# The last piece's keys in two halves of four steps, and the last half's store in three parts by lanes

## The chip, the cores and the metric

The kernel runs on one core of a Trainium2 chip (trn2). The metric is the device time of one execution in microseconds (us), before and after the change, as the median of several runs. A core has five engines with a queue of instructions each: TensorE (PE, matmuls and transposes), VectorE (DVE), ScalarE (ACT), GpSimd (POOL) and SyncE (SP, which here only starts DMA transfers). Each engine takes its instructions in order and waits on semaphores for the others.

## The reference

The computation has three stages, one behind the other. The change lies in the first.

```python
# attention-like recurrence: batch 4, 8 heads, 768 steps, head dimension 48; a = a_re + i*a_im
mag = sqrt(a_re^2 + a_im^2);  scale = min(mag, 0.999) / (mag + 1e-6);  a_n = a * scale
for t in range(768):
    S = a_n[t] * S            # complex, rows scaled
    S.re += outer(k[t], v[t])
    y[t] = q[t] @ S.re
# x = y as (3072 tokens, 384); then a mixture of 8 experts, top 1
e = argmax(x @ w_gate);  out = gate * (relu(x @ w1[e]) @ w2[e])
# then a gated product
h = (x @ w1) * (x @ w2);  out = (h @ w3) @ w_out
```

The kernel writes the recurrence in chunks of 64 steps. Within a chunk it takes the running products P of the decays; a query is multiplied by P and a key by the conjugate of P over |P|^2 (called "keys" here), so that a chunk becomes a masked product of queries and keys, and the state is carried from chunk to chunk.

## The kernel before

The 768 steps are three groups (g) of four chunks. 128 lanes hold 2 pairs of batches (q), 4 chunks (c), 8 heads and the 2 batches of a pair, in that order, so that 16 lanes belong to one (q, c). Two streams are written side by side by `drive`, which takes the next step of the stream that is behind in estimated time (the numbers that the steps yield).

**Stream 1, `elementwise`**, works on 24 pieces of 8 steps (`TP`), eight for each group; piece i covers 8 steps of all 128 lanes. For a piece: `root`, `excess` and `norm` make the scaled decays; `prefix` makes P one step after the other, each step a product (line 893, tile `pr`) and a sum (line 895, tile `P`) on DVE that needs the step before; `power` squares P on ACT (line 900, tile `s`); `weigh` adds the two squares (line 837, on DVE for the pieces of the last group) and takes 1/|P|^2 as Ln and Exp on ACT (lines 909, 910); `keys` multiplies on DVE (lines 918, 920, 922) and makes the tile `qk` with all products of a piece in one instruction of 1536 elements a lane (line 925). A piece's `qk` goes to `qkd` in HBM. The pieces that end a group (`LAST`: 7, 15, 23) are stored from SP in two halves of 64 lanes (line 934), the others from POOL (line 936). `keys` of a piece is written down two rounds after its `prefix`, except for a group's last piece, where it comes one round after it.

**Stream 2, `groups`**, works on units (g, q, c). `loads` (line 1027) reads a unit's 16 lanes and 64 steps back from `qkd` as tile `kk`, 768 KB in rows of 768 bytes; PE transposes it (line 1011, tile `tr`), multiplies it into scores and outputs (lines 1039, 1058, 1059), and carries the state in `W` (lines 1096, 1103). A group's first load needs the store of the group's last piece: `yield lambda: self.made > LAST[g]`. Behind it, when the units of a group have given their rows, `route` picks experts and scatters rows to HBM from POOL (line 162, after `pi` on DVE, line 157).

During the third group a side stream splits weights (`Fuse`, tiles `fdr`, `fdm`), which SP loads behind the first three `kk`. Then come the experts (lines 350 to 352, PE) and the last product.

Which instruction stands where in an engine's queue is settled when the program is built: a list scheduler with a model of time takes, for each engine, the earliest instruction in program order that is ready in the model. So an instruction that is written later can stand in a gap of one that is written earlier.

Of the kernel before, what the change touches and what calls it, by code (L numbers as in the profile page):

```python
# [9 lines left out]
F32 = mybir.dt.float32  # L10
# [4 lines left out]
AF = mybir.ActivationFunctionType  # L15
ALU = mybir.AluOpType
# [81 lines left out]
def bc(ap, n, at):  # L98
    shape = list(ap.shape)
    return ap.unsqueeze(at).to_broadcast(shape[:at] + [n] + shape[at:])  # L100
# [520 lines left out]
NH = 8  # L621
SEQ = 768
D = 48
C = 64
NG = 3
TP = 8
NPC = C // TP
NPIECE = NG * NPC
# [14 lines left out]
LAST = {g: max(r for r, x in enumerate(PAIRS) if g in [y[0] for y in x]) for g in range(NG)}  # L643
R2 = 2 * D
# [12 lines left out]
LAG = 5000  # L657
REST = 3
ZB = 4
HP = 1000  # L660


# [130 lines left out]
class Attn:  # L793
# [33 lines left out]
    def elementwise(self, aside, factors):  # L827

        nc, S, ep, e2 = self.nc, self.S, self.ep, self.e2
        v, act = nc.vector, nc.scalar  # L830
        E = TP * D
        td = lambda ap: ap.rearrange("p (t d) -> p t d", d=D)
        a, sq, pu, y0, cf, P, s2, px, raw = ({} for _ in range(9))

        def add(i, nm, s):
            if i not in ADDS[nm]:
                v.tensor_tensor(out=s[0], in0=s[0], in1=s[1], op=ALU.add)
                return s[0]
            p = self.adds.tile([128, 512], F32, tag="ad", name=f"{nm}{i}", bufs=2)[:, :E]
            for r in range(2):  # L840
                nc.tensor.matmul(p, S.ident, s[r], start=r == 0, stop=r == 1)  # L841
            return p

        def root(i):
            sq[i] = x = ep.tile([128, 2, E], F32, tag="sq", name=f"sq{i}", bufs=AHEAD)
            act.activation(out=x, in_=a[i], func=AF.Square, accum_out=S.su[:, i : i + 1])
            pu[i] = add(i, "u", (x[:, 0], x[:, 1]))
            y0[i] = y = ep.tile([128, E], F32, tag="y0", name=f"y0{i}", bufs=AHEAD)
            act.activation(out=y, in_=pu[i], func=AF.Ln, bias=S.tiny[:, 0:1])
            act.activation(out=y, in_=y, func=AF.Exp, scale=-0.5)  # L850
            act.activation(out=x[:, 1], in_=y, func=AF.Square, accum_out=S.sy[:, i : i + 1])

        def excess(i):
            v.tensor_tensor(out=sq[i][:, 0], in0=pu[i], in1=sq[i][:, 1], op=ALU.mult)
            yield 470

        def norm(i):
            u, y = sq[i][:, 0], y0[i]
            v.scalar_tensor_tensor(out=u, in0=u, scalar=3.0, in1=y, op0=ALU.subtract, op1=ALU.mult, reverse0=True)
            act.activation(out=y, in_=y, func=AF.Identity, scale=-0.4995e-6, bias=S.wb)  # L860
            yield 470
            v.scalar_tensor_tensor(out=u, in0=u, scalar=2.0 / 0.999, in1=y, op0=ALU.min, op1=ALU.mult)
            yield 470
            cf[i] = c = ep.tile([128, TP, 4, D], F32, tag="cf", name=f"cf{i}", bufs=2)
            ar = a[i].rearrange("p r (t d) -> p t r d", d=D)
            v.tensor_tensor(out=c[:, :, 0:3:2], in0=ar, in1=bc(td(u), 2, 2), op=ALU.mult)
            act.activation(out=c[:, :, 1], in_=c[:, :, 2], func=AF.Copy, scale=-1.0)
            act.copy(c[:, :, 3], c[:, :, 0])  # L868
            yield 870

        def prefix(i):
            P[i] = e2.tile([128, TP, 2, D], F32, tag="P", name=f"P{i}", bufs=3)
            m = len(PAIRS[i])
            n = TP // m
            run = lambda x: x.rearrange("p (m t) r d -> p m t r d", m=m)
            c, o = run(cf[i]), run(P[i])
            for t in range(n):
                k = [k for k in range(m) if t or PAIRS[i][k][1]]
                for x in range(m):
                    if x not in k:  # L880
                        v.tensor_copy(o[:, x, 0], c[:, x, 0, 0:3:2])
                        yield 120
                if not k:
                    continue
                if t:
                    pv = o[:, :, t - 1]
                else:
                    old = len(PAIRS[i - 1])
                    pv = P[i - 1].rearrange("p (m t) r d -> p m t r d", m=old)[:, old - len(k) :, TP // old - 1]
                j = len(k)  # L890
                pr = e2.tile([128, 2, 2, 2, D], F32, tag="pr", name=f"pr{i}_{t}", bufs=1)[:, :j]
                cx = c[:, :j, t].rearrange("p m (w r) d -> p m w r d", w=2)
                v.tensor_tensor(out=pr, in0=cx, in1=bc(pv, 2, 2), op=ALU.mult)  # L893
                yield 100 + 170 * j
                v.tensor_tensor(out=o[:, :j, t], in0=pr[:, :, :, 0], in1=pr[:, :, :, 1], op=ALU.add)
                yield 70 + 100 * j

        def power(i):
            s2[i] = e2.tile([128, 2, E], F32, tag="s2", name=f"s2_{i}", bufs=2)
            act.activation(out=s2[i].rearrange("p r (t d) -> p t r d", d=D), in_=P[i], func=AF.Square)  # L900
            g, _, n = PAIRS[i][0]
            if i == LAST[g]:
                self.last[g] = l = self.st.tile([128, 2, 2, D], F32, tag="td", name=f"td{g}")
                act.copy(l, P[i][:, n - 1].unsqueeze(2).to_broadcast([128, 2, 2, D]))

        def weigh(i):
            px[i] = add(i, "x", (s2[i][:, 0], s2[i][:, 1]))
            g0 = s2[i][:, 1]
            act.activation(out=g0, in_=px[i], func=AF.Ln, bias=S.tiny[:, 1:2])
            act.activation(out=g0, in_=g0, func=AF.Exp, scale=-1.0)  # L910

        def keys(i):
            g, _, n = PAIRS[i][0]
            k = raw[i][:, :, 1]
            x, g0 = s2[i][:, 0], s2[i][:, 1]
            if i == LAST[g]:
                v.tensor_copy(S.xm[:, g], px[i][:, (n - 1) * D : n * D])
            v.tensor_tensor(out=x, in0=px[i], in1=g0, op=ALU.mult)
            yield 470
            v.tensor_tensor(out=k, in0=k, in1=td(g0), op=ALU.mult)  # L920
            yield 470
            v.scalar_tensor_tensor(out=k, in0=td(x), scalar=2.0, in1=k, op0=ALU.subtract, op1=ALU.mult, reverse0=True)
            yield 470
            self.qk[i] = o = self.qp.tile([128, TP, 2, 2, D], F32, tag="qk", name=f"qk{i}")
            S.end = v.tensor_tensor(out=o, in0=bc(P[i], 2, 2), in1=bc(raw[i], 2, 3), op=ALU.mult)
            yield 1740
            self.stored = self.qk.pop(i).rearrange("p t w r d -> p (t w r d)")
            at = 0
            for g, t, n in PAIRS[i]:
                dst = S.qkd[g].rearrange("q c h b t w e -> (q c h b) t (w e)")[:, t : t + n].rearrange("l t e -> l (t e)")  # L930
                src = self.stored[:, at * 2 * R2 : (at + n) * 2 * R2]
                if i == LAST[g]:
                    for l in (0, 64):
                        done = nc.sync.dma_start(dst[l : l + 64], src[l : l + 64])
                else:
                    done = nc.gpsimd.dma_start(dst, src)
                at += n
            with self.tc.issue_after(done.ins):
                aside(i)
            self.made = i + 1  # L940
# [21 lines left out]
        yield from chain(excess(0), norm(0), excess(1))  # L962
        for i in range(NPIECE + 1):
            if i:
                power(i - 1)
                weigh(i - 1)
            if i % 2 and i + 5 < NPIECE:
                a[i + 5], a[i + 6] = self.load_a(i + 5)
            if i + AHEAD < NPIECE:
                root(i + AHEAD)  # L970
            if i + 1 < NPIECE:
                raw[i + 1] = self.load_qk(i + 1)
            ends = [j in LAST.values() for j in (i - 2, i - 1)]
            rest = [keys(i - 2)] if i > 1 and not ends[0] else []
            if i + 1 < NPIECE:
                rest.append(norm(i + 1))
            if ends[1]:
                rest.append(keys(i - 1))
            if i + 2 < NPIECE:
                rest.append(excess(i + 2))  # L980
            yield from mix(*([prefix(i)] if i < NPIECE else []), chain(*rest))
            if i == NPIECE - 1:
                factors()
# [92 lines left out]
    def chain(self, u, ld):  # L1076
# [8 lines left out]
        v, kk = ld  # L1085
        z = st.tile([R2, 2, HD], F32, tag="z", name=f"z{nm}", bufs=ZB)
        first = g == 0 and c == 0
# [27 lines left out]
    def fill(self, cost):  # L1115
# [3 lines left out]
        while self.pool and spent < cost:  # L1119
# [14 lines left out]
            try:  # L1134
                with self.tc.high_priority(HP) if self.spare is not None else nullcontext():
                    c = next(x.steps)
# [316 lines left out]
```

## Time and profile before

| | us |
|---|---|
| median of 3 runs | 996.49 |
| lowest, highest | 995.11, 997.68 |
| the profiled execution | 997.66 |
| its span, first to last instruction | 996.0 |
| PE busy in it | 885.2 (89%) |
| DVE busy | 609.6 (61%) |
| ACT busy | 496.2 (50%) |

All times within the trace count from the first instruction of the span. A busy share is an average over stages; a wait counts where PE, the busiest engine, stands still. In a row of a timeline the columns are start, duration, engine, line, operation, tile written and tiles read, partitions x elements, and the number of instructions merged into the row; brackets at the end give the engine's idle time before it and what ended that.

### The profile page before, as it was taken

Reading aid. Unit: us, or ns where it says so; the run is one execution under the profiler, and the core shown is the slowest. Engines: PE = TensorE matmul, PEld = TensorE weight load, DVE = VectorE, ACT = ScalarE, POOL = GpSimd, SP = SyncE. Lnnn points to the kernel's source line nnn. Section 1 sums busy time; section 2 is a strip of 40 time slices with the busy share of each in tenths; the row PEclk is TensorE's granted clock in tenths of the full one; section 3 lists DMA queues with packets and bytes.
Section 4 is the critical chain, followed back from the end, with each engine's and each line's share of the span. In section 5 each row is a group of like instructions: output and inputs, shape, how many; then the busy total and the mean of one; then the engine's idle time right before and its main releaser. Section 6 shows DMA issues by size and latency. Waiting matters only on the chain. (4 is left out here: it accounts for less than half of the span.)

```text
span 996.0 us, 17046 instructions
## 1 busy us (share of the span) xinstructions
PE 885.2 (89%) x6386; PEld 759.2 (76%) x6386; DVE 609.6 (61%) x1373; ACT 496.2 (50%) x1113; POOL 133.8 (13%) x194
## 2 busy tenths in 40 slices
PE   3535899879993898999989999998999999999997
PEld 1212478667873787989979999997888888888886
DVE  6999999888994795676489995443232323232222
ACT  7556699868862775344456654443131313131211
POOL 6111000202031011100233211110010100000001
PEclk9666899989995999899999999999999999999999
DMA  7556975476636872653678745630000000000000
GB/s 249 180 188 238 283 253 180 136 222 209 184 129 186 275 225 90 190 183 113 196 218 192 202 111 136 139 66 2 1 16 16 16 17 12 21 9 25 9 24 32
DMA packets 90183, 128.75 MB, mean 129 GB/s; under 512 B 7232, under 2 KB 72688, under 8 KB 90096
## 3 DMA queue, kind: packets, MB, share of 16 engines
q1 hardware_dynamic: 76540, 83.79, 29.8%
q0 software_dynamic: 10448, 39.18, 11.2%
q10 hardware_dynamic: 3108, 4.65, 1.5%
q8 instruction: 51, 0.84, 0.4%
q14 instruction: 36, 0.29, 0.1%
HBM read 92.38 MB, written 35.22 MB: 128 GB/s over the span
## 5 line engine op out<-in xcount | busy, mean ns | idle before, releaser
L606 DVE TENSOR_TENSOR ab<-asb,pb 128x512 f32<-128x512 f32 x48 | 33.0, 687 | 188.3 <-PE pb L352 183.5
L345 ACT CAST h<-w 128x384 fp32r<-128x384 f32 x128 | 65.0, 513 | 94.9 <-PE ph L351 44.8
L346 DVE TENSOR_TENSOR l<-w,h 128x384 fp32r<-128x384 f32 x128 | 70.5, 554 | 62.5 <-ACT h L345 59.1
L601 ACT COPY asb<-pa 128x512 f32<-128x512 f32 x48 | 28.1, 586 | 121.2 <-PE pa L352 116.7
L841 PE MATMUL x<-s,ident 128*128 128x384 f32 x64 | 36.5, 711 | 51.0 <-ACT s L900 51.0
L345 ACT CAST gh<-ab 128x512 fp32r<-128x512 f32 x48 | 29.7, 619 | 95.0 <-DVE ab L606 90.6
L1011 PE MATMUL tr<-ident,kk 128*96 128x128 f32 x384 | 57.9, 284 | 18.3 <-DMA kk<-qkd 18.3
L351 PE MATMUL py<-hl,h 128*128 128x432 f32 x192 | 69.9, 364 | 3.3 <-DVE hl L407 3.3
L350 PE MATMUL py<-hh,h 128*128 128x432 f32 x192 | 69.2, 360 | 1.9 <-ACT hh L406 1.9
L1012 ACT COPY qkT<-tr 96x512 f32<-96x512 f32 x96 | 54.6, 590 | 30.0 <-PE tr L1011 27.0
L350 PE MATMUL ph<-xh,h 128*128 128x432 f32 x192 | 69.0, 360 | 0.0
L352 PE MATMUL ph<-xh,l 128*128 128x432 f32 x192 | 69.0, 359 | 0.0
L893 DVE TENSOR_TENSOR pr<-cf,P 128x192 f32<-128x192 f32 x189 | 66.8, 353 | 3.4 <-ACT cf L868 0.3
L351 PE MATMUL ph<-xl,h 128*128 128x432 f32 x192 | 68.9, 359 | 0.0
L352 PE MATMUL py<-hh,l 128*128 128x432 f32 x192 | 68.9, 359 | 0.0
L570 POOL DMA_INDIRECT out<-ob,mdp x24 | 23.8, 992 | 306.5 <-DVE ob L569 164.7
L351 PE MATMUL po<-ol,gh 128*128 128x384 f32 x192 | 64.9, 338 | 0.0
L350 PE MATMUL po<-oh,gh 128*128 128x384 f32 x192 | 64.8, 337 | 0.0
L352 PE MATMUL po<-oh,gl 128*128 128x384 f32 x192 | 64.1, 338 | 0.0
L841 PEld LDWEIGHTS x<-s,ident 128*128 128x128 f32 x64 | 15.1, 259 | 63.9 <-ACT s L900 56.0
L1011 PEld LDWEIGHTS tr<-ident,kk 128*96 128x96 f32 x384 | 41.6, 130 | 26.5 <-issue 16.3
L350 PE MATMUL pa<-yh,ah 128*128 128x512 f32 x144 | 57.1, 396 | 3.0 <-ACT yh L345 3.0
(218 smaller groups left out, 2405.6 us busy)
## 6 DMA issues: line engine op xcount, KB each, us to landing
w<-in_w SPq DMA_DIRECT2D x128, 192.0 KB
kk<-qkd SPq DMA_DIRECT2D x24, 768.0 KB
qkd<-qk POOLq DMA_DIRECT2D x21, 768.0 KB
qkr<-in_qk SPq DMA_DIRECT2D x24, 384.0 KB
a<-in_a SPq DMA_DIRECT2D x11, 768.0 KB
fdr<-in_w SPq DMA_DIRECT2D x16, 512.0 KB
fdr<-in_v POOLq DMA_DIRECT2D x12, 512.0 KB
xs<-zr POOLq DMA_DIRECT2D x8, 648.0 KB
```

The costliest lines, as they stand in the source:

```text
L345: nc.scalar.copy(H, src)
L346: nc.vector.tensor_tensor(out=L, in0=src, in1=H.bitcast(F32), op=ALU.subtract)
L350: nc.tensor.matmul(out, lh, rh, start=first, stop=False)
L351: nc.tensor.matmul(out, lh, rl, start=False, stop=False)
L352: return nc.tensor.matmul(out, ll, rh, start=False, stop=last)
L570: nc.gpsimd.indirect_dma_start(out=S.outv[j], out_offset=bass.IndirectOffsetOnAxis(ap=S.mdp[:, j, 0:1], axis=0), in_=ob, in_offset=None, b ...
L601: nc.scalar.copy(asb, pa)
L606: nc.vector.tensor_tensor(out=ab, in0=asb, in1=pb, op=ALU.mult)
L841: nc.tensor.matmul(p, S.ident, s[r], start=r == 0, stop=r == 1)
L893: v.tensor_tensor(out=pr, in0=cx, in1=bc(pv, 2, 2), op=ALU.mult)
L1011: nc.tensor.transpose(pt[:, h], qk[:, h0 + h, w], self.S.ident)
L1012: nc.scalar.copy(qkT[:, w, h0 : h0 + 4], pt)
```

## The change

`CUTS` cuts the eight steps of a piece into two halves. For the last piece alone (i = 23): after step 3 of `prefix`, `power` and `weigh` are written for the first four steps; after `prefix`, for the last four. `keys` runs once for each half, on 192 elements a lane instead of 384, and 768 instead of 1536 for `qk`. The first half's `qk` is stored by one DMA of 128 lanes with 3072 bytes each; the last half's by three DMAs of 16, 48 and 64 lanes (`2 * NH` is 16), all from SP. The estimates that `keys` yields to `drive` stay what they were, and are now yielded for each half. All other pieces take the same instructions as before.

```diff
@@ -657,6 +657,7 @@
 LAG = 5000
 REST = 3
 ZB = 4
+CUTS = ((0, TP // 2), (TP // 2, TP))
 HP = 1000
 
 
@@ -893,38 +894,59 @@
                 v.tensor_tensor(out=pr, in0=cx, in1=bc(pv, 2, 2), op=ALU.mult)
                 yield 100 + 170 * j
                 v.tensor_tensor(out=o[:, :j, t], in0=pr[:, :, :, 0], in1=pr[:, :, :, 1], op=ALU.add)
+                if i == NPIECE - 1 and t == CUTS[0][1] - 1:
+                    power(i, CUTS[0])
+                    weigh(i, CUTS[0])
                 yield 70 + 100 * j
 
-        def power(i):
-            s2[i] = e2.tile([128, 2, E], F32, tag="s2", name=f"s2_{i}", bufs=2)
-            act.activation(out=s2[i].rearrange("p r (t d) -> p t r d", d=D), in_=P[i], func=AF.Square)
+        def cut(x, t):
+            return x[:, t[0] * D : t[1] * D]
+
+        def power(i, t=(0, TP)):
+            if not t[0]:
+                s2[i] = e2.tile([128, 2, E], F32, tag="s2", name=f"s2_{i}", bufs=2)
+            ts = slice(*t)
+            act.activation(out=s2[i].rearrange("p r (t d) -> p t r d", d=D)[:, ts], in_=P[i][:, ts], func=AF.Square)
             g, _, n = PAIRS[i][0]
-            if i == LAST[g]:
+            if i == LAST[g] and t[1] == TP:
                 self.last[g] = l = self.st.tile([128, 2, 2, D], F32, tag="td", name=f"td{g}")
                 act.copy(l, P[i][:, n - 1].unsqueeze(2).to_broadcast([128, 2, 2, D]))
 
-        def weigh(i):
-            px[i] = add(i, "x", (s2[i][:, 0], s2[i][:, 1]))
-            g0 = s2[i][:, 1]
-            act.activation(out=g0, in_=px[i], func=AF.Ln, bias=S.tiny[:, 1:2])
+        def weigh(i, t=(0, TP)):
+            px[i, t] = add(i, "x", (cut(s2[i][:, 0], t), cut(s2[i][:, 1], t)))
+            g0 = cut(s2[i][:, 1], t)
+            act.activation(out=g0, in_=px[i, t], func=AF.Ln, bias=S.tiny[:, 1:2])
             act.activation(out=g0, in_=g0, func=AF.Exp, scale=-1.0)
 
-        def keys(i):
+        def keys(i, t=(0, TP)):
             g, _, n = PAIRS[i][0]
-            k = raw[i][:, :, 1]
-            x, g0 = s2[i][:, 0], s2[i][:, 1]
-            if i == LAST[g]:
-                v.tensor_copy(S.xm[:, g], px[i][:, (n - 1) * D : n * D])
-            v.tensor_tensor(out=x, in0=px[i], in1=g0, op=ALU.mult)
+            ts = slice(*t)
+            k = raw[i][:, ts, 1]
+            x, g0 = cut(s2[i][:, 0], t), cut(s2[i][:, 1], t)
+            if i == LAST[g] and t[1] == TP:
+                v.tensor_copy(S.xm[:, g], px[i, t][:, (n - 1 - t[0]) * D : (n - t[0]) * D])
+            v.tensor_tensor(out=x, in0=px[i, t], in1=g0, op=ALU.mult)
             yield 470
             v.tensor_tensor(out=k, in0=k, in1=td(g0), op=ALU.mult)
             yield 470
             v.scalar_tensor_tensor(out=k, in0=td(x), scalar=2.0, in1=k, op0=ALU.subtract, op1=ALU.mult, reverse0=True)
             yield 470
-            self.qk[i] = o = self.qp.tile([128, TP, 2, 2, D], F32, tag="qk", name=f"qk{i}")
-            S.end = v.tensor_tensor(out=o, in0=bc(P[i], 2, 2), in1=bc(raw[i], 2, 3), op=ALU.mult)
+            if not t[0]:
+                self.qk[i] = self.qp.tile([128, TP, 2, 2, D], F32, tag="qk", name=f"qk{i}")
+            o = self.qk[i]
+            S.end = v.tensor_tensor(out=o[:, ts], in0=bc(P[i][:, ts], 2, 2), in1=bc(raw[i][:, ts], 2, 3), op=ALU.mult)
             yield 1740
-            self.stored = self.qk.pop(i).rearrange("p t w r d -> p (t w r d)")
+            self.stored = o.rearrange("p t w r d -> p (t w r d)")
+            if t != (0, TP):
+                dst = S.qkd[g].rearrange("q c h b t w e -> (q c h b) t (w e)")[:, C - TP + t[0] : C - TP + t[1]].rearrange("l t e -> l (t e)")
+                src = self.stored[:, t[0] * 2 * R2 : t[1] * 2 * R2]
+                if not t[0]:
+                    nc.sync.dma_start(dst, src)
+                    return
+                for l in ((0, 2 * NH), (2 * NH, 64), (64, 128)):
+                    done = nc.sync.dma_start(dst[slice(*l)], src[slice(*l)])
+                self.made = i + 1
+                return
             at = 0
             for g, t, n in PAIRS[i]:
                 dst = S.qkd[g].rearrange("q c h b t w e -> (q c h b) t (w e)")[:, t : t + n].rearrange("l t e -> l (t e)")
@@ -962,8 +984,9 @@
         yield from chain(excess(0), norm(0), excess(1))
         for i in range(NPIECE + 1):
             if i:
-                power(i - 1)
-                weigh(i - 1)
+                t = CUTS[1] if i == NPIECE else (0, TP)
+                power(i - 1, t)
+                weigh(i - 1, t)
             if i % 2 and i + 5 < NPIECE:
                 a[i + 5], a[i + 6] = self.load_a(i + 5)
             if i + AHEAD < NPIECE:
@@ -975,7 +998,7 @@
             if i + 1 < NPIECE:
                 rest.append(norm(i + 1))
             if ends[1]:
-                rest.append(keys(i - 1))
+                rest += [keys(i - 1, t) for t in (CUTS if i == NPIECE else ((0, TP),))]
             if i + 2 < NPIECE:
                 rest.append(excess(i + 2))
             yield from mix(*([prefix(i)] if i < NPIECE else []), chain(*rest))
```

## Rows read from the trace of the kernel before

**Rows 1.** The page: busy tenths and granted TensorE clock in 40 slices of 24.9 us.

```profile
PE   3535899879993898999989999998999999999997
PEclk9666899989995999899999999999999999999999
```

**Rows 2.** Windows of the span: busy us (and instructions) of each engine, clock, DMA share, GB/s.

```profile
core 0: us, PE busy (x) PEld busy (x) DVE busy (x) ACT busy (x) POOL busy (x), PEclk, DMA share, GB/s
309.00:321.40 12.40, 0.00 (x0) 0.00 (x0) 1.27 (x6) 0.00 (x0) 3.95 (x4) 0.50 0.80 231
321.40:330.00 8.60, 7.10 (x74) 6.23 (x74) 2.37 (x6) 5.34 (x15) 0.00 (x0) 0.84 1.06 380
330.00:680.00 350.00, 338.74 (x2463) 314.99 (x2464) 244.78 (x536) 192.68 (x419) 56.46 (x53) 0.99 0.58 159
```

**Rows 3.** Timeline of PE around the start of the third group.

```profile
306.94 1.43 PE L151 MATMUL rk<-oh,ones 128*128 128x24 f32 x6
321.45 0.85 PE L1011 MATMUL tr<-ident,kk 128*96 128x128 f32 x3 [13.07 <-DMA kk<-qkd]
```

**Rows 4.** Timeline of SP's queue (DMA issues) at the same place.

```profile
309.73 1.11 SPq L934 DMA_DIRECT2D qkd<-qk  x2
313.50 5.03 SPq L1027 DMA_DIRECT2D kk<-qkd  x3
```

**Rows 5.** Timeline of DVE from step 3 of the last piece to the scatter's indices.

```profile
296.42 0.26 DVE L895 TENSOR_TENSOR P<-pr 128x96 f32<-128x96 f32 x1
...
297.80 0.94 DVE L1112 TENSOR_TENSOR ca<-W,T 96x768 f32<-96x768 f32 x1
...
300.50 0.35 DVE L893 TENSOR_TENSOR pr<-cf,P 128x192 f32<-128x192 f32 x1
300.77 1.75 DVE L925 TENSOR_TENSOR qk<-P,qkr 128x1536 f32<-128x1536 f32 x1
...
303.11 0.26 DVE L895 TENSOR_TENSOR P<-pr 128x96 f32<-128x96 f32 x1
304.28 0.56 DVE L837 TENSOR_TENSOR s<-s 128x384 f32<-128x384 f32 x1 [0.91 <-ACT s L900]
...
306.25 0.56 DVE L918 TENSOR_TENSOR s<-s 128x384 f32<-128x384 f32 x1
...
307.95 1.75 DVE L925 TENSOR_TENSOR qk<-P,qkr 128x1536 f32<-128x1536 f32 x1
...
310.13 0.17 DVE L157 CAST pi<-pos 128x4 int32<-128x4 f32 x1
```

**Rows 6.** Timeline of ACT behind the last step of P.

```profile
303.40 0.84 ACT L900 ACTIVATE s<-P 128x768 f32<-128x768 f32 x1 [0.47 <-DVE P L895]
304.15 0.33 ACT L904 COPY td<-P 128x192 f32<-128x192 f32 x1
...
304.87 0.61 ACT L909 ACTIVATE s<-s,tiny 128x384 f32<-128x384 f32 x1 [0.32 <-DVE s L837]
...
305.70 0.53 ACT L910 ACTIVATE s<-s 128x384 f32<-128x384 f32 x1
```

**Rows 7.** Short windows behind the store's issue (columns as in rows 2).

```profile
309.73:310.50 0.77, 0.00 (x0) 0.00 (x0) 0.54 (x5) 0.00 (x0) 0.00 (x0) 0.50 0.00 0
310.50:311.00 0.50, 0.00 (x0) 0.00 (x0) 0.00 (x0) 0.00 (x0) 0.00 (x0) 0.50 0.76 172
311.00:312.50 1.50, 0.00 (x0) 0.00 (x0) 0.00 (x0) 0.00 (x0) 1.11 (x2) 0.50 1.03 201
312.50:313.50 1.00, 0.00 (x0) 0.00 (x0) 0.00 (x0) 0.00 (x0) 0.90 (x1) 0.50 0.79 240
```

**Rows 8.** Timeline of SP and PE where the second group starts.

```profile
211.19 3.94 SPq L1027 DMA_DIRECT2D kk<-qkd  x3
217.85 1.94 PE L1011 MATMUL tr<-ident,kk 128*96 128x128 f32 x8 [5.18 <-DMA kk<-qkd]
```

**Rows 9.** Timeline of POOL: the scatters of the second group's rows.

```profile
311.08 1.01 POOL L162 DMA_INDIRECT xs<-xo,pi  x1 [7.74 <-DVE pi L157]
```

## The prediction, on record before the change was run

> **What bounds the kernel now.** The page comes first, to see which engine is the busiest and where it is not. PE's slices are at eight tenths and more nearly everywhere behind the middle; the hole is slice 13, three tenths, at a granted clock near half [rows 1]. The windows give its edges: from 309.00 to 321.40 PE does nothing, and from 330 to 680 it is busy 338.74 of 350 us, so that whatever stands behind the hole is PE's own work and moves with its start [rows 2]. PE's timeline names what ends the hole: the transposes of the third group's first unit begin at 321.45, having waited 13.07 us for the load of `kk` [rows 3]. That load is one link of a chain that the timelines of the other engines give: the last step of P ends at 303.37 on DVE; squares, sum, Ln and Exp alternate between ACT and DVE until 306.23; three products and the large one end at 309.70 [rows 5, 6]; SP issues the two halves of the store at 309.73 and the first load at 313.50 [rows 4]; 7.95 us later PE starts. From P to PE that is 6.33 + 0.03 + 3.77 + 7.95 = 18.08 us. DVE, not PE, is the busy engine just ahead of 303.37, and the other group's PE work has run out by 308.37 [rows 3, 5]. So the change works on a chain that sets the end, and a microsecond taken from it is a microsecond of the kernel if the rest keeps its order.
>
> **The tail of the chain on half a piece.** Behind P's last step only four steps' keys are left. No row shows such halves, so each is priced by the nearest row of the same size. Before: 6.33 us. After: the squares fall from 768 elements to 384, which the Exp of that size does in 0.53; the sum falls to 192 elements, 0.35 by the product `pr`; Ln and Exp lose the 0.20 that lies between the Exp of 384 (0.53) and the copy of 192 (0.33), so 0.41 and 0.33 [rows 5, 6]. Three DVE products of 192 elements follow one another every 0.27 us (300.50 to 300.77, the `pr` and what stands behind it), and the large one, 768 elements, takes 0.95 by the 0.94 of the instruction on 768 elements [rows 5]. The gaps between them in the old chain stay: 0.03, 0.04, 0.03, 0.22, 0.02 and 0.13 between the last short product and the large one. Sum: 0.53 + 0.35 + 0.41 + 0.33 + 3 x 0.27 + 0.95 + 0.47 = 3.85 us, a saving of 2.48.
>
> **What the first half puts ahead of it.** The first half's work is all added on busy engines before P is done. Its squares can start when step 3 ends, 296.68 [rows 5]. Its DVE part is one sum and three products at 0.27 and a large product of 0.86 to 0.95 less overlap (the next instruction starts 1.67 us into a 1.75 us one): 0.27 + 0.81 + 0.87 = 1.95 us. DVE is in use from 296.68 to 303.37, also with the keys of the piece before, whose large product runs at 300.77 [rows 5]. Whatever of the 1.95 us stands ahead of P's step 7 delays the tail; whatever stands behind it hides in the time in which DVE waits for ACT, which is 0.91 us idle ahead of the sum now, and the 1.41 between the sum's end (304.84) and the first product (306.25), filled today with small routing work that nothing near waits for [rows 5]. The sum is written ahead of steps 4 to 7, so its 0.27 counts for certain; the keys are written behind them and can only take gaps. Bounds: 0.27 and 1.95. I take 0.9, the sum, two short products in the two waits around step 7, and a little for the large one standing ahead of the second sum, which is nearer to the lower end because the small work can give way. If the cover were gone, the tail would come 1.05 us later than that. Net: the tail ends 1.6 us earlier (0.5 to 2.2), at about 308.1.
>
> **The store.** Added: one DMA of 384 KB early, and three in place of two at the end. Each issue costs SP about 0.55 us (1.11 for two [rows 4]). The early one is off the path: it needs what the old store of 384 KB needed until the load's issue, 3.77 us at most, and can go at 305 to 306; nothing else is in SP's queue there until 309.73, so it is done by 309.8. Of the last three, SP passes the third at 1.65 us behind the first, and the first load waits behind them. How long it waits is read thus: no byte moves until 310.50, and 86 KB by 311.00, which at 201 GB/s puts the start at 0.9 us behind the issue; then 393 KB of the first 64 lanes need 1.96 us; the remaining 0.91 is the way back to SP [rows 7]. By 313.50 the DMA engines had moved 86 + 301 + 240 = 627 KB of the 786 KB of both halves, so the load was let go before the second half of the lanes had landed [rows 4, 7]: the wait is by lanes. With 16 lanes of 3072 bytes, 49 KB, the data term falls to 0.24 us and the issue-to-issue time to 0.9 + 0.24 + 0.91 = 2.05 us, above SP's 1.65. Saving 1.7. Bounds: 1.9 if the way back shrinks with the size as well, and -0.5 if the load waits for the last part after all, since all parts hold the same 393 KB as one old half and one more issue is in front.
>
> The Trainium skill (DMA: Bandwidth & Descriptors, section Rules for kernel authors) speaks against this edit: transfers to disjoint parts of the partitions run one after the other on the same engines and should be one transfer, and below 64 KB one pays mostly overhead. The rows above bear out the overhead, 1.81 of 2.05 us; what the rule leaves out is who waits, and the trace shows a wait for a part. By the rule alone the store's term would be nothing or worse, which is the second rival.
>
> **The load.** It takes 7.95 us from issue to PE here, and 6.66 us where the second group starts [rows 3, 4, 8]. Here the scatters of four tiles, 786 KB, start at 311.08 and share the engines [rows 9]. They hang on `pi`, which ran right behind the large product at 310.13 [rows 5], so they too will come earlier by one to two us and meet the load again. The rest of the store, 344 KB or 1.7 us, is through by the time the load's first bytes can move. I take a gain of 0.4; bounds 1.3 (no scatter) and -1.0 (about a third of the scatters' 3.4 us at 231 GB/s [rows 2] comes on top).
>
> **What is late next.** The second unit's load is right behind and has the DMA engines at full share (1.06, 380 GB/s [rows 2]): 786 KB take 2.1 us, while PE has the first unit's work to do. The clock was at 0.50 through the hole and averages 0.84 up to 330 [rows 2]; a hole of nine us instead of thirteen is still a hole, so PE restarts at 1.2 GHz as before, and nothing is counted for it.
>
> **Sum.** 1.6 + 1.7 + 0.4 = 3.7 us. The profiled execution took 997.66, 1.17 above the median of 996.49; from its own time it gives 994.0, and from the median **992.8 us**. About 0.3%, 3.0 us, is what a measurement of this kernel can tell from no change, so the forecast is just past it.
>
> **Rivals.**
>
> *The first half only pushes the tail.* All 1.95 us stand ahead of P's end because DVE has no gap there. The tail's gain is 2.48 - 1.95 = 0.5, the store gives 1.7, the load nothing: 2.2 us, 994.3. For it: DVE shows only short gaps from 296.68 on [rows 5]. Against: keys are written behind P's steps and give way to them.
>
> *The parts give nothing.* The load waits for the last part, -0.5; with 1.6 and 0.4 that is 1.5 us, 995.0. For it: three issues on one queue and the same bytes. Against: the 627 KB.
>
> *The order behind the hole gets worse.* `drive` now counts the keys' 3150 twice, and every queue is planned again. From 330 to 680 PE stands idle 11.26 us in all [rows 2]. If the new order lengthened that by six tenths, 6.8 us, the result would be 996.49 + 6.8 - 3.7 = 999.6; it decides the sign from 3.7 us, a third more, on. For it: DVE and ACT are well used there (244.78 and 192.68 of 350). Against: stream 2 has nothing left to write in the time that is added, since its PE work had ended by 308.37 [rows 3].
>
> **How the numbers follow.** The forecast holds gains of 3.0 to 5.5 us, 0.62. The first rival has 0.18, the second 0.08, the third 0.09; 0.03 is left for no change at all through a cause that I do not see. That gives faster 0.62, within 0.3% 0.29, slower 0.09. The upper terms together, 2.2 + 1.9 + 1.3, are 5.4, so 991.1, and a little for the run-to-run spread of 1.3 us puts the low end at 990.3. The high end takes in the first two rivals and stops at 996.0.
>
> **What would show it.** PE's first `tr` of the third group at 317 to 318 instead of 321.45, its idle time 9 to 10 us instead of 13.07; P's last step at 303.8 to 304.8; the last large product of 768 elements ending near 308.1; a load of `kk` issued about 2 us behind the first small store. If P's last step ends past 305, the first rival holds; if the load is issued 3.5 us or more behind the store, the second; if PE starts early and the end does not follow, the third. I am wrong if the hole shrinks by less than 3 us, or if PE's idle time between 330 and 680 grows.

## The result and the profile after

The changed kernel took 988.63 us, the kernel before 998.49 us in the same comparison (six runs each); the ratio is 0.9919, 95% interval 0.9899 to 0.994. Two later comparisons gave 0.990 (0.9882 to 0.9919) and 0.9904 (0.9885 to 0.9923). The sign and the place were forecast; the size was not: 0.37% was forecast and 0.8 to 1.0% came. The forecast's range ended at 990.3 us. The ratio times its median of 996.49 gives 988.4 (986.4 to 990.5), which is below the range but for the edge of the interval.

The page of the changed kernel, busy tenths and clock in slices of 24.7 us:

```profile
PE   3645899979984999999899999998999999999997
PEclk9676999979996999999989999998999999999999
```

The hole in slice 13 is smaller than in [rows 1], four tenths instead of three. The windows give its length, 7.4 us of no PE work where there were 12.4 [rows 2]:

```profile
core 0: us, PE busy (x) PEld busy (x) DVE busy (x) ACT busy (x) POOL busy (x), PEclk, DMA share, GB/s
304.20:311.60 7.40, 0.00 (x1) 0.00 (x0) 0.57 (x6) 0.00 (x0) 3.96 (x4) 0.50 0.78 223
```

Timeline of DVE in the changed kernel, from P's last step to the scatter's indices:

```profile
299.36 0.25 DVE L896 TENSOR_TENSOR P<-pr 128x96 f32<-128x96 f32 x1
299.53 0.95 DVE L937 TENSOR_TENSOR qk<-P,qkr 128x768 f32<-128x768 f32 x1
...
300.49 0.34 DVE L838 TENSOR_TENSOR s<-s 128x192 f32<-128x192 f32 x1
...
302.13 0.35 DVE L928 TENSOR_TENSOR s<-s 128x192 f32<-128x192 f32 x1
...
303.18 0.96 DVE L937 TENSOR_TENSOR qk<-P,qkr 128x768 f32<-128x768 f32 x1
...
304.64 0.17 DVE L157 CAST pi<-pos 128x4 int32<-128x4 f32 x1
```

Timeline of ACT in it:

```profile
299.64 0.52 ACT L909 ACTIVATE s<-P 128x384 f32<-128x384 f32 x1 [2.12 <-DVE P L896]
...
300.87 0.45 ACT L918 ACTIVATE s<-s,tiny 128x192 f32<-128x192 f32 x1 [0.47 <-DVE s L838]
...
301.54 0.36 ACT L919 ACTIVATE s<-s 128x192 f32<-128x192 f32 x1
```

Timelines of SP, PE and POOL in it:

```profile
300.50 0.33 SPq L944 DMA_DIRECT2D qkd<-qk  x1
304.17 1.33 SPq L947 DMA_DIRECT2D qkd<-qk  x3
306.00 2.82 SPq L1050 DMA_DIRECT2D kk<-qkd  x3
...
311.67 0.64 PE L1034 MATMUL tr<-ident,kk 128*96 128x128 f32 x2 [7.46 <-DMA kk<-qkd]
...
305.59 1.01 POOL L162 DMA_INDIRECT xs<-xo,pi  x1 [6.57 <-DVE pi L157]
```

Read against [rows 3 to 6]: the tail, from P's end to the end of the large product, is 4.53 us (299.61 to 304.14) instead of 6.33; the load is issued 1.83 us behind the store instead of 3.77; PE starts 5.67 us behind the load instead of 7.95. From P's end to PE that is 12.06 us instead of 18.08. PE starts 9.78 us earlier than before, but of these 4.60 were there already ahead of the change: the scaling of the state, 297.80 in [rows 5], stands at 293.20 in this profile, although DVE, ACT and POOL do the same work in the same order up to there. And of the 9.78 the end keeps only 6.6 (span 989.4 instead of 996.0). So one pair of profiles doesn't tell how much the change gives. The experiments take each kernel's time apart at four points of the trace: the scaling of the state (`ca`, DVE), the end of P's step 7, the third group's first transpose, and the first matmul behind the third group (`Wf`, PE).

### The profile page after: what moved, and what is told of

It is laid out like the page before. It is cut to its first block, busy times and chain, and to the rows that moved or that the text cites. A ratio compares the mean times of both kernels' runs of the same rounds, so it can differ in the third digit from the quotient of the medians.

```text
span 989.4 us, 17064 instructions
## 1 busy us (share of the span) xinstructions
PE 889.9 (90%) x6386; PEld 760.8 (77%) x6386; DVE 609.6 (62%) x1378; ACT 497.4 (50%) x1116; POOL 130.9 (13%) x194
```

## The experiments

All numbers of this table are differences of times in each kernel's timelines, in us. "State to PE" is the stretch that the change is written for; "third group" goes from PE's first transpose to the first `Wf`; "rest" from there to the span's end.

| kernel | tail | store to load | load to PE | state to PE | third group | rest |
|---|---|---|---|---|---|---|
| before | 6.33 | 3.77 | 7.95 | 23.65 | 82.08 | 592.5 |
| before, again | 6.33 | 3.77 | 7.61 | 23.31 | 83.94 | 594.0 |
| changed | 4.53 | 1.83 | 5.67 | 18.47 | 77.66 | 600.1 |
| changed, again | 4.53 | 1.84 | 5.75 | 18.56 | 77.23 | 596.0 |
| changed, third | 4.53 | 1.83 | 5.86 | 18.66 | 77.21 | 596.3 |
| halves only | 4.54 | 2.73 | 5.31 | 19.00 | 83.33 | 596.0 |
| parts only | 6.33 | 2.59 | 8.53 | 23.04 | 90.46 | 593.0 |
| estimates halved | 4.53 | 1.83 | 5.65 | 18.44 | 83.91 | 595.2 |
| estimates doubled | 6.33 | 3.77 | 8.35 | 24.05 | 76.70 | 598.5 |
| before, no scatters | 6.33 | 3.77 | 5.54 | 21.24 | 80.73 | 594.7 |
| changed, no scatters | 4.53 | 1.83 | 4.86 | 17.65 | 76.88 | 594.2 |
| late store | 4.53 | 2.54 | 8.21 | 21.72 | 85.50 | 593.5 |
| cut behind step 5 | 4.25 | 1.72 | 5.33 | 17.94 | 77.75 | 595.0 |

The profile of the parts alone is of an execution of 1007.19 us, 5.4 us above the median of its twelve. The two kernels without scatters (992.98 and 983.09 us, beside a median of 996.71 of the kernel before) and the late store were run once each.

**Both kernels again.** No edit; a second profile of each, on one chip.

> The kernel before, a second profile of it, to see what repeats. Theory A (the chain from the last step of P to the third group's first transpose sets the gain): that chain takes 18.1 us again within 0.5, and the stretch from the first transpose to the first expert matmul 82.1 us within 1. Theory B (the third group's new order is worth as much as the chain): the same numbers for this kernel, since the order is the same. Theory C (much of the difference is how long the first 300 us take from run to run): the landmark ahead of the change, the product that scales the state at the end of the second group, moves by several us from its 297.80. Ratio 1.00 within 0.3% by all.

> The changed kernel, a second profile. A: from the last step of P to the first transpose 12.0 us within 0.5. B: from the first transpose to the first expert matmul 77.7 us within 1, 4.4 less than before. C: the landmark ahead of the change is not 4.6 us earlier than in the kernel before again. Ratio 0.991 to 0.993 by A and B; nearer to 0.995 if C made half of the difference.

Measured: 1.000 (0.9986 to 1.0014) and 0.990 (0.9882 to 0.9919). Timelines of DVE and PE, the kernel before:

```profile
298.08 0.94 DVE L1112 TENSOR_TENSOR ca<-W,T 96x768 f32<-96x768 f32 x1
...
321.39 1.91 PE L1011 MATMUL tr<-ident,kk 128*96 128x128 f32 x8 [12.73 <-DMA kk<-qkd]
...
398.78 2.05 PE L1096 MATMUL W<-cb,perm 96*96 96x384 f32 x4 [3.09 <-DVE W L1112]
...
405.33 0.69 PE L350 MATMUL Wf<-woh,w3h 128*128 128x384 f32 x1
```

and the changed one:

```profile
299.41 0.94 DVE L1135 TENSOR_TENSOR ca<-W,T 96x768 f32<-96x768 f32 x1
...
317.97 1.27 PE L1034 MATMUL tr<-ident,kk 128*96 128x128 f32 x5 [7.56 <-DMA kk<-qkd]
...
395.20 0.44 PE L350 MATMUL Wf<-woh,w3h 128*128 128x384 f32 x1
```

Here the changed kernel is 1.33 us *later* at the state's scaling, so the 4.60 us of the first pair do not come from the change. The spans, 999.3 and 991.2, differ by 8.1: + 1.33 ahead of the change, - 4.75 from there to PE, - 6.71 in the third group, + 2.03 behind it. The largest term is one that the forecast doesn't have.

**The two edits apart.** First the halves without the three parts, against the changed kernel:

```diff
-                for l in ((0, 2 * NH), (2 * NH, 64), (64, 128)):
+                for l in ((0, 64), (64, 128)):
```

> The two halves of four steps stay, the last half is stored in two parts of 64 lanes. A: the tail behind P stays 1.8 us shorter, the step from store to load takes 2.8 us (half of the 64 lanes' bytes of before) where the change has 1.83 and before 3.77; the time is 1 to 2 us above the changed kernel, ratio 0.993 to 0.994. B: the third group has yet another order here, so its length can be anything between 77 and 83 us, and the ratio follows it: 0.990 to 0.998.

Measured: 0.9987 (0.9973 to 1.0). SP's and PE's timelines:

```profile
308.71 1.11 SPq L947 DMA_DIRECT2D qkd<-qk  x2
311.44 1.07 SPq L1050 DMA_DIRECT2D kk<-qkd  x2
...
316.75 1.49 PE L1034 MATMUL tr<-ident,kk 128*96 128x128 f32 x6 [8.00 <-DMA kk<-qkd]
...
400.08 0.44 PE L350 MATMUL Wf<-woh,w3h 128*128 128x384 f32 x1
```

Then the three parts without the halves, in the kernel before:

```diff
-                    for l in (0, 64):
-                        done = nc.sync.dma_start(dst[l : l + 64], src[l : l + 64])
+                    for l in ((0, 2 * NH), (2 * NH, 64), (64, 128)) if i == NPIECE - 1 else ((0, 64), (64, 128)):
+                        done = nc.sync.dma_start(dst[slice(*l)], src[slice(*l)])
```

> The last piece's keys stay whole; only its store is cut into 16, 48 and 64 lanes of 6144 bytes. A: the tail behind P is 6.33 us as before, the step from store to load falls from 3.77 to about 2.3 us, the load takes 7 to 8 us; 1.5 to 2 us gained, ratio 0.998 to 0.9985. B: the same chain, but the length of the third group changes with its order, 77 to 83 us, so 0.993 to 0.999. If the load waits for all parts, the step takes 4.3 us and A gives 1.000.

Measured: 0.9999 (0.9979 to 1.0019). SP and PE:

```profile
310.87 1.33 SPq L934 DMA_DIRECT2D qkd<-qk  x3
313.46 8.34 SPq L1027 DMA_DIRECT2D kk<-qkd  x4
...
321.99 1.91 PE L1011 MATMUL tr<-ident,kk 128*96 128x128 f32 x8 [12.46 <-DMA kk<-qkd]
```

Two things follow. The chain behaves as the sum of its edits, but not as the forecast shared it out: the halves alone take store-to-PE from 11.4 to 11.7 us down to 8.04, the parts alone to 11.12, both together to 7.50. The parts free the load 1.2 us earlier, and the load gives most of it back (8.53 us to PE). And the times don't follow the chain: with halves alone PE starts 4.3 to 4.7 us earlier, counted from the state's scaling, and the kernel gains 0.13%, with an interval that reaches 1.0. Beside the second profile of the kernel before, on the same chip, its span is 3.2 us shorter (996.1 and 999.3): 0.33 ahead of the change, 4.31 from there to PE and 0.61 in the third group, less 2.05 that the rest is longer. What it lacks against the changed kernel is the shorter third group, 83.33 us where that has 77.23. Of these 6.1 us, 4.1 are busy time of PE (78.36 and 74.22 us). Windows of the kernel with halves only show where PE is slow:

```profile
324.00:332.00 8.00, 6.99 (x49) 4.88 (x50) 5.08 (x12) 3.61 (x10) 0.00 (x0) 0.57 1.01 311
332.00:365.00 33.00, 32.67 (x524) 27.94 (x521) 27.79 (x73) 27.33 (x69) 2.69 (x2) 1.00 0.73 229
365.00:377.00 12.00, 11.37 (x101) 9.20 (x103) 11.25 (x29) 5.69 (x13) 0.00 (x0) 0.57 0.45 132
```

The granted clock averages 0.57 in two windows of 8 and 12 us, so that PE runs at the lower of its two levels, 1.2 GHz, for most of them; it is 1.00 between them. The columns are those of [rows 2]. Both kernels missed both of their expected ranges, and each has a third group in an order of its own, neither the one before nor the changed one. So their times don't price the two edits; the chain's stretches do.

**Chain and order apart.** The planned queues of these kernels differ in the whole third group, not just at the change. The cause is in the program's writing. `keys` yields its estimates once for each half, so `drive` counts 6300 ns for the last piece instead of 3150, and gives stream 2 three more turns before the third group begins. A line that prints stream 2's pool at that moment, while the program is built, says:

```
before    pool=[('route', 233, True)] turns=233
changed   pool=[] turns=236
```

So before, one route of the second group was still unfinished, and every later choice of the next step stood elsewhere. That allows a clean pair of kernels, and the traces bear it out: set side by side, PE's instructions of the third group differ in 43 places between the kernel before and the changed one. With the estimates halved they differ from the kernel before's in 2 places, as those of its second profile do; with the estimates doubled they are the changed kernel's. The counting is not all that sets the order: the kernel with halves only counts the same 6300 ns and has another one. One kernel of the pair is the whole change, with the estimates cut to a half's share (excerpt against the changed kernel):

```diff
+            w = (t[1] - t[0]) / TP
-            yield 470
+            yield 470 * w
...
-            yield 1740
+            yield 1740 * w
```

> The whole change, but the keys' estimates for stream 2's turn are cut in proportion to a half's size, so that they add up to what they were before. PE's queue is then the one of the kernel before but for two places ahead of the third group. A (the chain alone): the chain from P's last step to the first transpose is 12.1 us and the ratio stays 0.990. B (chain and order are worth about five us each): the chain is 12.1 us, 5 us gained net of P's delay, the stretch from the first transpose to the end of the third group is 82 to 84 us as before with its 3.1 us wait near the end, and the ratio is 0.995. C (variation of the first 300 us): no difference from the changed kernel.

The other is the kernel before with only the estimates doubled for the last piece (`w = 2 if i == NPIECE - 1 else 1`, and the same four yields times `w`).

> The kernel before with nothing but the last piece's estimates doubled, as the change does it by counting them for each half. Its third group has the order of the changed kernel but for 7 places. A: ratio 1.000. B: the chain takes 17.9 us as before, the third group 77.5 us instead of 83, and the ratio is 0.994 to 0.995. C: 1.000.

Measured: 0.9961 (0.9945 to 0.9978) for the change with the old order, 0.997 (0.9948 to 0.9993) for the old chain with the new order. PE's timeline of the first:

```profile
310.69 1.70 PE L1035 MATMUL tr<-ident,kk 128*96 128x128 f32 x7 [7.45 <-DMA kk<-qkd]
...
387.25 2.85 PE L1120 MATMUL W<-cb,perm 96*96 96x384 f32 x4 [3.08 <-DVE W L1136]
...
394.60 0.69 PE L350 MATMUL Wf<-woh,w3h 128*128 128x384 f32 x1
```

and of the second:

```profile
316.81 1.49 PE L1012 MATMUL tr<-ident,kk 128*96 128x128 f32 x6 [13.34 <-DMA kk<-qkd]
...
393.51 0.44 PE L350 MATMUL Wf<-woh,w3h 128*128 128x384 f32 x1
```

With the old order the last carry of the state waits 3.08 us for DVE (3.09 in the kernel before), since nothing is left on PE to stand in front of it; with the new order the outputs of a unit stand there, and in the changed kernel the same wait is 0.31 us:

```profile
384.22 1.50 PE L1119 MATMUL W<-cb,perm 96*96 96x384 f32 x4 [0.31 <-DVE W L1135]
```

The first `Wf` takes 0.69 us behind the old order and 0.44 behind the new one: behind the wait PE also runs at 1.2 GHz for a while (in the kernel before's second profile the granted clock is 0.50 from 400 to 405 and 0.89 in the mean from 390 to 420; in the changed kernel's first it is 1.00 from 390 to 420). The chain alone gives 0.39% (0.22 to 0.55), the order alone 0.3% (0.07 to 0.52), and neither reaches the 0.8 to 1.0% of both. The pair was measured on one chip, the two later comparisons of the whole change on two others. The order alone gives less than its expected 0.994 to 0.995: its third group is as short as expected, 76.70 us, but the rest is 598.5.

**What the load waits for.** The same four scatters, those of the second group's last rows, left out of either kernel:

```diff
-    for i, x in enumerate(xtiles):
+    for i, x in enumerate(xtiles if slot0 != 12 else []):
```

> The kernel before without the four scatters of the second group's last rows (those rows are missing from the output). If the scatters make the load slow, the load of the third group's first unit takes 6.0 to 6.7 us from issue to PE instead of 7.6 to 7.95. If the load waits on its rings behind the store's 786 KB, it still takes over 7 us.

> The changed kernel without the same four scatters (those rows are missing from the output). If the scatters are what the load loses time to, it takes 4.5 to 5 us from issue to PE instead of 5.7. If the remaining 344 KB of store ahead of it set its start, it stays at 5.5 to 5.8 us.

Load and transpose, kernel before without them:

```profile
310.27 2.59 SPq L1027 DMA_DIRECT2D kk<-qkd  x3
...
315.81 1.49 PE L1011 MATMUL tr<-ident,kk 128*96 128x128 f32 x6 [10.67 <-DMA kk<-qkd]
```

and the changed kernel without them:

```profile
305.45 2.43 SPq L1050 DMA_DIRECT2D kk<-qkd  x3
...
310.31 1.49 PE L1034 MATMUL tr<-ident,kk 128*96 128x128 f32 x6 [6.65 <-DMA kk<-qkd]
```

The load takes 5.54 us instead of 7.6 to 7.95 in the one, 4.86 instead of 5.7 to 5.9 in the other: the scatters cost 2.1 to 2.4 us before and 0.8 to 1.0 after. The 5.54 is below the 6.0 to 6.7 that was expected. Before, the load is issued 2.42 us behind the first scatter (313.50 and 311.08), after the change 0.41 us behind it (306.00 and 305.59). The packets in the traces say what that does: before, the scatters' first bytes move 0.47 us behind the load's issue and ahead of any of the load's; after, 3.08 us behind it, when 418 rows of 768 bytes have started (a unit has 1024). Without any scatter, the change still takes 2.62 us off the way from store to PE (9.31 to 6.69).

The other half of the question is the store's own bytes. Keys in halves, but the whole piece stored at the end in the three parts (against the changed kernel, shortened at `...`):

```diff
                 if not t[0]:
-                    nc.sync.dma_start(dst, src)
                     return
+                dst = S.qkd[g].rearrange(...)[:, C - TP : C].rearrange("l t e -> l (t e)")
+                src = self.stored
```

> The keys in two halves as in the change, but nothing is stored early: the whole piece goes at the end in parts of 16, 48 and 64 lanes with 6144 bytes a lane, 786 KB instead of 393. If the bytes that stand on the rings ahead of the load set its start, the tail behind P stays 4.53 us, the load is issued 2.6 us behind the store, and takes 7.5 to 8.5 us to PE, as where only the parts were made; from store to transpose 10.5 to 11 us instead of 7.5. If the scatters alone make the load slow, the load takes 5.7 us as in the changed kernel.

SP and PE:

```profile
309.11 1.33 SPq L948 DMA_DIRECT2D qkd<-qk  x3
311.65 8.60 SPq L1051 DMA_DIRECT2D kk<-qkd  x4
...
319.86 1.49 PE L1035 MATMUL tr<-ident,kk 128*96 128x128 f32 x6 [10.72 <-DMA kk<-qkd]
```

One run, 1000.59 beside a median of 1001.56 of the kernel before. Store to PE takes 10.75 us, 3.25 more than with the first half stored early; the tail is the change's. The load of 8.21 us is near that of the parts alone (8.53). The place of the scatters doesn't explain it. Their first, on POOL, with halves only and with the late store:

```profile
310.14 1.01 POOL L162 DMA_INDIRECT xs<-xo,pi  x1 [6.57 <-DVE pi L157]
310.53 1.01 POOL L162 DMA_INDIRECT xs<-xo,pi  x1 [6.57 <-DVE pi L157]
```

The load is issued 1.30 us behind it with halves only and takes 5.31 us, and 1.12 us behind it here. What differs is the store: its last bytes move until 3.41 us behind the load's issue here, and until 0.14 with halves only and 1.24 in the changed kernel. Where the load is let go early, it has the rest of the store ahead of it. The Trainium skill (DMA: Bandwidth & Descriptors, section Queues, rings and completion order) says that an engine takes a ring's descriptors in order. The two runs fit that, but they don't show it ring by ring; and since the scatters share the engines in them, how much of the 3.25 us is the store's bytes alone is not separated.

**Another cut.** `CUTS = ((0, 5), (5, TP))`, beside the changed kernel on one chip.

> The change with the cut behind step 5 instead of 4; PE's queue keeps the changed kernel's order but for 6 places. The last store shrinks to 295 KB, 0.5 us less on the rings, and the tail's short instructions save some 0.4 us; against it, the first part's keys, 1.25 times as long, start one step later and no longer fit ahead of the tail, which costs up to 0.8 us. From P's step to the first transpose 11.3 to 12.5 us, ratio 0.988 to 0.992, the changed kernel's within what can be told.

> The changed kernel a third time, beside the cut behind step 5 on the same chip. By chain and order together: the chain 12.1 us, the third group 77 to 78 us, ratio 0.990 to 0.993. If the order's part were chance, the third group would be 82 to 84 us this time.

Measured: 0.9905 (0.9881 to 0.993) and 0.9904 (0.9885 to 0.9923). The cut behind step 5, SP and PE:

```profile
307.01 1.33 SPq L947 DMA_DIRECT2D qkd<-qk  x3
308.73 2.96 SPq L1050 DMA_DIRECT2D kk<-qkd  x3
...
314.06 1.27 PE L1034 MATMUL tr<-ident,kk 128*96 128x128 f32 x5 [6.58 <-DMA kk<-qkd]
```

and the changed kernel for the third time:

```profile
318.58 1.70 PE L1034 MATMUL tr<-ident,kk 128*96 128x128 f32 x7 [7.65 <-DMA kk<-qkd]
...
395.79 0.44 PE L350 MATMUL Wf<-woh,w3h 128*128 128x384 f32 x1
```

The stretch from the state's scaling to PE is 0.5 to 0.7 us shorter, and the times don't tell it. The third group took 77.2 us a third time, so its length belongs to its order: with the changed kernel's order it is 76.70 to 77.75 us, with that of the kernel before 80.73 to 83.94. The halves alone, the parts alone and the late store have other orders and 83.33, 90.46 and 85.50 us.

## Why the prediction was right in sign and wrong in size

- **What bounds the kernel.** Right. PE's start of the third group waits for the chain, and with the order held the change gives 0.39% (3.9 us, interval 2.2 to 5.5) for 4.9 to 5.2 us of chain (18.44 against 23.31 to 23.65).
- **The first half ahead of P.** Right: 0.9 us was taken, and P's step 7 ends 6.41 us behind the state's scaling instead of 5.57, so 0.84. The keys went into the gaps, and the large product fell behind step 7.
- **The tail.** Mis-sized: a saving of 2.48 was put, 1.80 came. The instructions have nearly the lengths that were put (0.52, 0.34, 0.45, 0.36, 0.35, 0.96); the gaps, which were put as in the old chain, grew. The second sum begins at 300.49, 0.33 us behind the squares' end, because the first half's large product holds DVE until then. Small routing work stands on DVE ahead of the first short product, 0.23 us behind the Exp, and between the last ones.
- **The store.** The term of 1.7 came as 1.94 (3.77 to 1.83), and the wait is by lanes (2.59 us with the parts alone). But what it buys was mis-stated. With the halves in place the parts free the load 0.90 us earlier (2.73 to 1.83), and the load gives back 0.36 of it (5.31 to 5.67). Alone they take 0.3 to 0.6 us off store-to-PE, since the load has the rest of the store ahead of it. What counts is that half of the bytes have left the path: stored late, that half costs 3.25 us, with the scatters beside it. The second rival, drawn from the rule of the Trainium skill (DMA: Bandwidth & Descriptors, Rules for kernel authors), is thus nearer to the truth for this edit taken alone than the forecast's term, though not for the reason given there: the load was let go early and took longer. (The measured 0.9999 holds another order as well.)
- **The load.** Mis-sized: 0.4 was put, 1.75 to 2.3 came (5.67 to 5.86 against 7.61 and 7.95). The step that failed here is that the scatters "will come earlier by one to two us and meet the load again". They come earlier by their own chain, the load by two us more, so that three to four tenths of a unit's rows (304 to 418 in four profiles with the change) have started before the scatters' first bytes, where before none had. That is worth 1.1 to 1.6 us (the scatters' cost before less that after), and 0.7 are left without any scatter (5.54 to 4.86).
- **The order.** This is the step that failed by most, a term put at nothing: "stream 2 has nothing left to write in the time that is added". It had one unfinished route, which does not show as work in PE's last rows ahead of the hole but decides the turn of all later steps. The third rival named the place and had the sign wrong: the third group got shorter by 4.4 to 6.7 us, not longer. It isn't all kept: the order alone measures 0.3%, about 3 us. The rest is longer in most kernels with this order (595.0 to 600.1 us) than in those with the old one (592.5, 594.0, and 595.2 with the estimates halved), but the ranges touch, and without scatters there is no such difference (594.2 and 594.7). Where the gain is lost was not settled. The sign that the prediction named, PE's idle time from 330 to 680, reads both ways, since the window covers other work in each profile: 13.25 us against 11.26 in the first pair, 9.15 against 11.31 in the second.
- **First rival.** Fell: P's step 7 moved by 0.84, not 1.95.

The chain's terms add up to 5 us, the order to 3, and the measured difference is 8 to 10; the intervals are too wide to say whether anything is left over.

## What to carry to other kernels

Where a program is laid out by a planner that counts estimates, look for what an edit does to the counting itself, and test it by changing the estimates alone: here that was about a third of the gain, by 0.3% with an interval from 0.07 to 0.52. The two edits taken apart gave 0.13% and nothing, each with yet another order behind it, so such times don't price an edit. A store that a load waits for costs twice, once until its completion and once as bytes ahead of the load; here moving half of it out of the way early was worth 3.25 us, letting the load go earlier only about half a us. Before counting on a saved wait, ask when the transfers that share the engines will come relative to the one that gains.

## What the runs showed that was not expected

DVE and POOL do the same instructions in the same order up to the state's scaling in all kernels here, and yet reach it at 292.25 to 299.92 us (estimates halved, and the changed kernel for the third time), as much as the whole gain. Much of that goes with the chip: on one chip it lies at 292.25 to 294.57, on the two others at 297.75 to 299.41 and 296.12 to 299.92, and the kernel before has a median of 996.71 us on the first and of 1001.71 and 1001.56 on the others. A single pair of profiles misleads unless it is of one chip and the time is taken apart at a point ahead of the change.

And the clock can take back an early start. In the one profile of the kernel with halves only, the mean granted clock of the third group is 0.87, where the changed kernel's third group has 0.97 and 0.98 (0.95 and 0.96 before); with the parts alone it is 0.86. PE is busy for 78.36 us in the third group of the halves, and for 73.57 and 74.22 in the changed kernel's. The first of its two slow stretches follows a wait of 2.73 us of PE for ACT. Whether that comes with the order of those kernels or with the execution is not shown.
